# A speech joint network's forward and backward pass: gradient rows transposed by DMA, one weight-gradient tap moved an iteration on, row loads on another queue

## The chip, the cores and the metric

The kernel runs on one core of one Trainium2 chip. The metric is device time in microseconds (us) of one execution; lower is better. The engines are named as in the profile: PE is TensorE (PEld its weight loads), DVE VectorE, ACT ScalarE, POOL GpSimd, SP SyncE. SP computes nothing here and issues DMAs. A DMA that SP issues and one that POOL issues go through different queues (in the profile q1 hardware_dynamic and q0 software_dynamic).

## The reference

Two strided convolutions with gelu, a projection, and a joint over U = 8 label positions; the outputs are the forward result and the gradients of all seven inputs. B = 2, T = 16000, D = 256, three taps, all bf16.

```python
def _fwd_reference(x, w1, w2, g, w_f, w_g, w_o):
    ...
    h = _gelu(h)[:, ::2, :]          # h: three taps of x with w1
    ...
    f = _gelu(f)[:, ::2, :]          # f: three taps of h with w2
    fe = jnp.einsum("btd,de->bte", f, w_f)
    ge = jnp.einsum("bud,de->bue", g, w_g)
    j = jnp.tanh(fe[:, :, None, :] + ge[:, None, :, :])
    return jnp.einsum("btud,dv->btuv", j, w_o)

def reference(x, w1, w2, g, w_f, w_g, w_o, grad_out):
    ...
    _out, _vjp = jax.vjp(_f, x, w1, w2, g, w_f, w_g, w_o)
    _grads = _vjp(grad_out)
    _out0 = jnp.asarray(_out)
    return (_out0, *[jnp.asarray(_g) for _g in _grads])
```

The gradient through the tanh, summed over the eight label positions, is what the rest of the backward pass starts from. The kernel keeps it with its sign turned and calls it NGFE.

## The kernel before

**Tiling.** Time after both strides has 4000 positions per batch. Both batches stand one after the other in one axis with a gap of 16, cut into 16 chunks of 512 columns (the last has 336; the eighth, n = 7, holds the end of the first batch and the start of the second, so each of its transfers falls into several pieces). Channels lie on partitions, 2 x 128.

**The main loop** runs over the chunks n. One iteration does three things at once: the joint of chunk n (four steps of two label positions each), the two convolutions and the projection of chunk n + 1, and the backward pass of chunk n - 1. The joint is the generator `main`; the other two are chained into the generator `fill`, and `weave` takes one unit of `fill` after nearly every unit of `main`. A scheduler then orders each engine's instructions, mostly along that order. After the loop the backward pass of the last chunk runs alone.

**The joint.** `gj` squares the tanh (ACT), multiplies grad_out, transposed (tile GOT), by w_o (PE, L635) and makes the gradient NGZ of one label position (DVE, L639, three buffers). `ngfe_acc` sums the NGZ on POOL (L658); the eighth sum is written as NGFE (one buffer). `o_block` is the forward matmul (L695), its result OUT is copied by ACT and stored by POOL's queue (L722). `gwo` is the gradient of w_o (L734): it needs the tanh with time on partitions (JR, transposed by a DMA of SP's queue, L667, two buffers) and grad_out's rows (GO, loaded by SP's queue in `load_go`, L202, three buffers). Both are asked for at a step's start or end and read one step after their own joint.

**The backward pass of a chunk**, in order: `d1_units` multiplies NGFE by w_f (L431) and makes GF (DVE, L433). `row_units` transposes what the weight gradients need with time on partitions: first NGFE (8 matmuls against the identity into one PSUM bank, L467, one DVE copy, L469), then four sets of 6 or 8 (HT and GF, copied by ACT). `d5_units` goes back through w2 (L454) and makes GH. `braid` alternates the two, beginning with the NGFE unit. `gwf_units` is the w_f gradient (L512; its rows are FR, transposed by DMA, and the NGFE rows), `gw2_units` that of w2 (L530). `ghr_units` transposes GH (16 matmuls, L467). `e_units` makes the x gradient (`gx_block`, L590, four per chunk, copied to GX by ACT, stored by POOL) and the three taps of the w1 gradient (`gw1`, 16 matmuls each, L603). `gw1` reads the GH rows and XR, rows of x that POOL's queue loads (`load_xr`, L213, one buffer, four pieces in the first two steps of the next iteration). The third tap stands between the third and the fourth `gx_block`, at the end of the iteration.

**Buffers.** Pool `rowp` (five buffers, tile "rows") holds the NGFE rows, the four HT/GF sets and the two GH sets of a chunk in turn.

**Queues.** SP's and POOL's instructions run in order, so a DMA issue that waits for a buffer or for data holds up all that is behind it in its queue. POOL's queue mixes sums, small copies, stores and loads.

Of the kernel before, what the change touches and what calls it, by code (L numbers as in the profile page):

```python
# [13 lines left out]
BF16 = mybir.dt.bfloat16  # L14
# [8 lines left out]
P = 128  # L23
KT = 2
KK = 3
# [3 lines left out]
CW = 512  # L29
# [3 lines left out]
def kernel(  # L33
# [30 lines left out]
    def geom(n):  # L64
        c0 = n * CW
        return c0, min(CW, L - c0)
# [43 lines left out]
    accp = pool("accp", 1)  # L110
    gfp = pool("gfp", 2)
    ghp = pool("ghp", 2)
    rowp = pool("rowp", 5)
    xrp = pool("xrp", 1)
    gxp = pool("gxp", 2)
    jtp = pool("jtp", 4)
# [75 lines left out]
    def joint_dram(t, b, q, m, up, nb):  # L192
        src = t[b, q:q + m, 2 * up:2 * up + 2, :]
        return src.rearrange("(tb p) u v -> p tb (u v)", tb=nb)

    def load_go(n, up):
        t = gop.tile([P, 4, 2 * V], BF16, name="GO")
        for lo, hi in gaps(n):
            p0 = lo % P // 32 * 32
            nc.vector.memset(t[p0:-(-(hi % P) // 32) * 32, lo // P, :], 0.0)  # L200
        for b, q, m, p0, p1, k, nb in joint_rows(n):
            nc.sync.dma_start(out=t[p0:p1, k:k + nb, :], in_=joint_dram(grad_out, b, q, m, up, nb))  # L202
        S[n]["GO", up] = t


# [257 lines left out]
    def transposes(srcs, dsts, evict=None):  # L463
# [4 lines left out]
        for dst, M, j0, j1 in dsts:  # L468
            (evict or nc.vector.tensor_copy)(out=dst, in_=ps[:M, j0:j1, :])  # L469

    def load_fr(n):
        W = geom(n)[1]
        FR = frp.tile([P, KT, 4, P], BF16, name="FR")
        nc.sync.dma_start_transpose(out=FR[:].rearrange("p k a d -> p (k a) d"),
                                    in_=S[n]["FT"][:].rearrange("p k w -> p (k w)"))
        S[n]["FR"] = FR

    def row_units(n):
        c0, W = geom(n)
        st = S[n]  # L480
        HT, GF, FT, NG = st["HT"], st["GF"], st["FT"], st["NGFE"]
        bl = blocks(W)
        FR = st["FR"]
        t = rowp.tile([P, 8, P], BF16, name="rows")
        st["NR"] = t
        srcs = [(NG[:, kt, o:o + M], 2 * j + kt, M) for j, (o, M) in enumerate(bl) for kt in range(KT)]
        dsts = [(t[:M, 2 * j:2 * j + 2, :], M, 2 * j, 2 * j + 2) for j, (o, M) in enumerate(bl)]
        if W == CW:
            dsts = [(t[:], P, 0, 8)]
        transposes(srcs, dsts)  # L490
        yield
        st["HG"] = []
        s = nsets(n)
        for k, M in sets(n):
            t = rowp.tile([P, 8, P], BF16, name="rows")
            col = lambda off: slice(off + k, off + k + s * (M - 1) + 1, s)
            srcs = [(HT[:, par, kt, col(2)], 2 * par + kt, M) for par in range(2) for kt in range(KT)]
            srcs += [(GF[:, kt, col(2)], 4 + kt, M) for kt in range(KT)]
            if k == 0:
                srcs += [(HT[:, 1, kt, col(1)], 6 + kt, M) for kt in range(KT)]  # L500
            transposes(srcs, [(t[:M, 0:len(srcs)], M, 0, len(srcs))], nc.scalar.copy)
            st["HG"].append(t)
            yield

    def gwf_units(n):
        W = geom(n)[1]
        FR, t = S[n]["FR"], S[n]["NR"]
        bl = blocks(W)
        ps = ps_f32()
        for k, (o, M) in enumerate(bl):  # L510
            for dt in range(KT):
                nc.tensor.matmul(ps[:, dt * D:(dt + 1) * D], lhsT=FR[:M, dt, k, :],  # L512
                                 rhs=t[:M, 2 * k:2 * k + 2, :].rearrange("p k d -> p (k d)"),
                                 start=(k == 0 and dt == 0), stop=(k == len(bl) - 1 and dt == KT - 1))
        flush("F", ACCF[:], ps[:])
        first_flush["F"] = False
        yield
# [17 lines left out]
        first_flush["2"] = False  # L535

    def braid(rows, d5):
        for gen in (rows, d5, rows, d5, rows, d5, rows, rows, d5):
            yield next(gen, None)

    def alternate(a, b):
# [31 lines left out]
    def e_units(n):  # L573
        st = S[n]
        s = nsets(n)
        GH, GR, XR = st["GH"], st["GR"], st["XR"]
        bl = back_sets(n)

        def gx_block(k, M):
            t = gxp.tile([P, 4, D], BF16, name="GX")  # L580
            combos = (((0, 1, 0), (2, 0, -1)), ((1, 1, 0),), ((2, 1, 0), (0, 0, 0)), ((1, 0, 0),))
            for cp in range(2):
                ps = ps_f32()
                for cj in range(2):
                    cc = combos[2 * cp + cj]
                    j, last = 0, len(cc) * KT - 1
                    for (i, par, sh) in cc:
                        for kt in range(KT):
                            o = 2 + k + sh
                            nc.tensor.matmul(ps[:M, cj * D:(cj + 1) * D], lhsT=GH[:, par, kt, o:o + s * (M - 1) + 1:s],  # L590
                                             rhs=W1T[:, i, kt, :], start=(j == 0), stop=(j == last))
                            j += 1
                nc.scalar.copy(out=t[:M, 2 * cp:2 * cp + 2, :], in_=ps[:M, :])  # L593
                yield
            store_gx(n, k, t)

        def gw1(i):
            ps = ps_f32()
            for j, (k, M) in enumerate(bl):
                t, g = GR[j]  # L600
                for dt in range(KT):
                    for par in range(2):
                        nc.tensor.matmul(ps[:, dt * D:(dt + 1) * D],  # L603
                                         lhsT=XR[:M, 4 * k + i + 2 * (1 - par), dt * P:(dt + 1) * P],
                                         rhs=t[:M, g + 2 * par:g + 2 * par + 2, :].rearrange("p k d -> p (k d)"),
                                         start=(j == 0 and dt == 0 and par == 0),
                                         stop=(j == len(bl) - 1 and dt == KT - 1 and par == 1))
            flush("1", ACC1[:, i, :], ps[:])

        for j, (k, M) in enumerate(bl):  # L610
            yield from gx_block(k, M)
            if j < KK:
                gw1(j)
                yield
        first_flush["1"] = False


# [206 lines left out]
        tanh(0, u)  # L824
    load_jr(0, 0)

    for n in range(G):
        back, fwd = n > 0, n + 1 < G
        conv = conv_units(n + 1) if fwd else iter(())
        conv2 = conv2_units(n + 1) if fwd else iter(())  # L830
        late_open[0] = False
        parts = []
        if back:
            d1, e, rows, ghr = d1_units(n - 1), e_units(n - 1), row_units(n - 1), ghr_units(n - 1)
            parts += [islice(conv, 2), islice(d1, 1), islice(conv, 1), d1, conv, braid(rows, d5_units(n - 1)),
                      gwf_units(n - 1), gw2_units(n - 1), islice(ghr, 1), islice(conv2, 1), ghr, conv2, islice(e, 6)]
            if fwd:
                parts.append(fe_units(n + 1))
            parts.append(e)
        else:  # L840
            parts += [conv, empty(3), islice(conv2, 1), empty(3), conv2, empty(3), fe_units(n + 1)]
        fill = chain(*parts)
        ratio = (0.92 if n > 0 else 0.4) if n + 1 < G else 0.72
        for up in range(U // 2):
            step = n * (U // 2) + up
            if step + 2 < len(orderp):
                load_got(*orderp[step + 2])
            if step + 1 < len(orderp):
                load_go(*orderp[step + 1])
            if up == 1:  # L850
                load_fr(n)
            for piece in (((0,), (1,), (2, 3), ()) if n == G - 1 else ((0, 1), (2, 3), (), ()))[up] if back else ():
                load_xr(n - 1, piece)
            main = joint_units(n, up)
            weave(main, fill, ratio)
            if up == U // 2 - 1:
                for _ in fill:
                    pump(2)
                    pump_late(1)
                pump(len(later))  # L860
                late_open[0] = True
                pump_late(len(late))
            for i in range(2):
                if 2 * step + 2 + i < len(order):
                    tanh(*order[2 * step + 2 + i])
            if step + 1 < len(orderp):
                load_jr(*orderp[step + 1])
            if n + 2 < G:
                load_x(n + 2, ((0,), (1,), (), ())[up])
# [2 lines left out]
        gwo(*prev_gwo[0], k)  # L872
    for piece in range(4):
        load_xr(n, piece)
    for _ in chain(d1_units(n), alternate(row_units(n), d5_units(n)), gwf_units(n), gw2_units(n), ghr_units(n), e_units(n)):
        pass


# [71 lines left out]
```

## Time and profile before

| | us |
|---|---|
| median of 3 runs | 839.2 |
| lowest, highest | 837.9, 847.22 |
| the profiled execution | 834.64 |
| its span in the profile | 832.7 |

| Group (line, engine) | count | mean ns of one | busy us |
|---|---|---|---|
| L734 PE, w_o gradient | 1008 | 274 | 150.0 |
| L695 PE, forward joint | 1008 | 274 | 148.7 |
| L603 PE, w1 gradient | 756 | 273 | 90.4 |
| L467 PE, transposes of NGFE | 126 | 219 | 9.6 |
| L469 DVE, copies of transposes | 51 | 647 | 32.7 |
| L658 POOL, sums | 80 | 2111 | 168.9 |
| L722 POOL, OUT stores | 76 | 737 | 55.9 |

| DMA | issuer | size KB | median us from issue to landing |
|---|---|---|---|
| GO | SP | 512 | 5.4 |
| GOT, transposing | SP | | 7.7 |
| JR, transposing | SP | | 6.8 |
| FR, transposing | SP | | 4.5 |
| XR | POOL | 256 | 7.1 |
| OUT | POOL | 512 | 6.0 |

How to read it: matmuls are pipelined, so the mean duration of one (274 ns) is longer than the distance from one to the next, and the chain of waits, which counts from start to start, gives four L734 matmuls 0.44 us and eight transposes 0.45 us. A DMA's landing is counted from its issue. An issue's own duration is the time that its queue is taken. Small groups and the waits' releasers are inferred from semaphores.

### The profile page before, as it was taken

To read this page: it belongs to the slowest core of one execution; us is meant where nothing else is said; L and a number is where in the kernel's file an instruction comes from. 1 tells how busy PE (TensorE), PEld (TensorE's weight loads), DVE (VectorE), ACT (ScalarE), POOL (GpSimd) and SP (SyncE) were. 2 spreads that over 40 slices of the span, in tenths; PEclk is the share of its full clock that TensorE was granted. 3 is DMA by queue.
4 is the path that set the end of the run, shared out by engine and by line. 5 is a ranking of instruction groups with operands and counts; after the bars stand their busy time and mean duration, and the time that the engine had idled before them with its cause. 6 is when DMAs were issued, how large, how long until landed. Compare 5 with 4: busy or idle time off the path is not lost.

```text
span 832.7 us, 16683 instructions
## 1 busy us (share of the span) xinstructions
PE 809.9 (97%) x6396; PEld 600.1 (72%) x6396; DVE 627.5 (75%) x1211; ACT 678.8 (82%) x1080; POOL 402.0 (48%) x423
## 2 busy tenths in 40 slices
PE   7979999999999999999999999999999999999797
PEld 3546777768678676777768678677777868778596
DVE  4896797886869778696877869778696886878344
ACT  3889998796979969799797979969798896978344
POOL 1154644454544535545477545535544454556371
PEclk9999999999999999999999999999999999999999
DMA  9878999999999999999999999999999999998954
GB/s 215 193 180 185 221 223 264 224 254 231 246 245 221 195 250 246 238 240 194 231 246 248 264 235 260 254 230 245 220 246 230 233 252 240 224 230 186 213 139 131
DMA packets 395344, 187.88 MB, mean 226 GB/s; under 512 B 343296, under 2 KB 379032, under 8 KB 395264
## 3 DMA queue, kind: packets, MB, share of 16 engines
q1 hardware_dynamic: 374944, 119.69, 77.3%
q0 software_dynamic: 20320, 67.12, 26.1%
q8 instruction: 50, 0.82, 0.4%
q14 instruction: 30, 0.25, 0.1%
HBM read 51.38 MB, written 50.34 MB: 122 GB/s over the span
## 4 chain that ended last, share of the span: by engine, by line
PE 84%; ACT 6%; DVE 5%; DMA 3%; issue 1%; POOL 0%; POOLq 0%; DVEq 0%; ACTq 0%
PE GWO_ps L734 12%; PE ps L695 11%; PE ps L635 11%; PE ps L603 9%; PE ps L590 9%; PE ps L324 7%; PE ps L530 5%; PE pst L467 5%; PE ps L359 5%; PE ps L454 4%; DMA JR<-JT 3%; PE ps L512 2%; ACT JT L401 2%; PE ps L383 2%; PE ps L431 1%; DVE g_s L264 1%
## 5 line engine op out<-in xcount | busy, mean ns | idle before, releaser
L639 DVE SCALAR_TENSOR_TENSOR NGZ<-JSQ,ps 128x512 bf16<-128x512 bf16 (+3 forms) x272 | 168.1, 639 | 45.1 <-PE ps L635 39.3
L658 POOL TENSOR_TENSOR ACCN<-ACCN,NGZ 128x1024 f32<-128x1024 f32 (+1 forms) x80 | 168.9, 2111 | 68.0 <-DVE NGZ L639 67.2
L697 ACT CAST OUT<-ps 128x512 bf16<-128x512 f32 (+1 forms) x252 | 146.1, 596 | 41.2 <-PE ps L695 36.0
L401 ACT ACTIVATE JT<-FE,GE 128x512 bf16<-128x512 f32 (+3 forms) x272 | 176.8, 710 | 0.5
L627 ACT ACTIVATE JSQ<-JT 128x1024 bf16<-128x1024 bf16 (+1 forms) x128 | 135.1, 1059 | 37.8 <-DVE NGZ L639 37.8
L734 PE MATMUL GWO_ps<-GO,JR 128*128 128x256 bf16 (+1 forms) x1008 | 150.0, 274 | 7.8 <-DMA JR<-JT 5.7
L695 PE MATMUL ps<-WO,JT 128*128 128x256 bf16 (+1 forms) x1008 | 148.7, 274 | 0.0
L722 POOL DMA_DIRECT2D out_dram<-OUT x76 | 55.9, 737 | 183.5 <-ACT OUT L697 171.2
L635 PE MATMUL ps<-GOT,WOT 128*128 128x512 bf16 (+1 forms) x512 | 139.0, 376 | 0.0
L734 PEld LDWEIGHTS <-JR 128*128 128x128 bf16 (+1 forms) x1008 | 97.3, 98 | 34.8 <-DMA JR<-JT 6.4
L695 PEld LDWEIGHTS <-JT 128*128 128x128 bf16 (+1 forms) x1008 | 98.0, 99 | 21.6 <-issue 1.3
L590 PE MATMUL ps<-W1T,GH 128*128 128x256 bf16 (+2 forms) x756 | 100.4, 273 | 0.0
L590 PEld LDWEIGHTS <-GH 128*128 128x128 bf16 (+2 forms) x756 | 83.5, 116 | 13.0
L324 PE MATMUL ps<-XC,W 128*128 128x512 bf16 (+1 forms) x384 | 91.1, 375 | 0.0
L603 PE MATMUL ps<-rows,XR 128*128 128x256 bf16 (+1 forms) x756 | 90.4, 273 | 0.0
L415 DVE TENSOR_TENSOR ACC<-ACC,ps 128x512 f32<-128x512 f32 x90 | 61.5, 684 | 37.9 <-PE ps L530 26.4
L264 DVE SCALAR_TENSOR_TENSOR g_s<-g_sq,g_x 128x1024 bf16<-128x1024 bf16 (+2 forms) x35 | 69.9, 1998 | 25.3 <-ACT g_sq L264 25.3
L603 PEld LDWEIGHTS <-XR 128*128 128x128 bf16 (+1 forms) x756 | 73.9, 98 | 11.6
L593 ACT CAST GX<-ps 128x512 bf16<-128x512 f32 (+2 forms) x126 | 72.3, 588 | 11.2 <-PE ps L590 4.8
L245 POOL DMA_DIRECT2D out_dram<-GX x67 | 36.8, 550 | 82.7 <-ACT GX L593 77.7
L635 PEld LDWEIGHTS <-WOT 128*128 128x128 bf16 x512 | 48.4, 98 | 32.4 <-issue 0.8
L324 PEld LDWEIGHTS <-W 128*128 128x128 bf16 x384 | 37.4, 98 | 37.3
(132 smaller groups left out, 1235.4 us busy)
## 6 DMA issues: line engine op xcount, KB each, us to landing
GO<-in_grad_out_dram SPq DMA_DIRECT2D x56, 512.0 KB, 5.4
out_dram<-OUT POOLq DMA_DIRECT2D x56, 512.0 KB, 6.0
out_dram<-GX POOLq DMA_DIRECT2D x55, 256.0 KB, 4.6
XR<-in_x_dram POOLq DMA_DIRECT2D x39, 256.0 KB, 7.1
XR<-in_x_dram POOLq DMA_DIRECT2D x13, 320.0 KB, 7.6
GO<-in_grad_out_dram SPq DMA_DIRECT2D x4, 384.0 KB, 4.1
out_dram<-OUT POOLq DMA_DIRECT2D x4, 384.0 KB, 6.1
GOT<-in_grad_out_dram SPq DMA_TRANSPOSE x68, 7.7
```

The costliest lines, as they stand in the source:

```text
L264: later.popleft()()
L324: nc.tensor.matmul(ps[:, :W], lhsT=W1[:, i, kt, mt * P:(mt + 1) * P], rhs=st["X", c][:, kt, 16 + sh:16 + sh + W], start=(k == 0), stop=(k ...
L401: act = nc.scalar.activation(out=JT[:, mt, lo:hi], in_=S[n]["FE"][:, mt, lo:hi], func=ACT.Tanh, bias=GE[:, b, mt, u:u + 1], scale=1.0)
L590: nc.tensor.matmul(ps[:M, cj * D:(cj + 1) * D], lhsT=GH[:, par, kt, o:o + s * (M - 1) + 1:s], rhs=W1T[:, i, kt, :], start=(j == 0), stop=( ...
L603: nc.tensor.matmul(ps[:, dt * D:(dt + 1) * D], lhsT=XR[:M, 4 * k + i + 2 * (1 - par), dt * P:(dt + 1) * P], rhs=t[:M, g + 2 * par:g + 2 * ...
L627: jsq = nc.scalar.activation(out=JSQ[:, :, :W], in_=JT[:, :, :W], func=ACT.Square)
L635: nc.tensor.matmul(ps[:, :W], lhsT=WOT[:, kt, mt * P:(mt + 1) * P], rhs=GOT[:, kt, :W], start=(kt == 0), stop=(kt == KT - 1))
L639: nc.vector.scalar_tensor_tensor(out=NGZ[:, mt, lo:hi], in0=JSQ[:, mt, lo:hi], scalar=1.0, in1=ps[:, lo:hi], op0=ALU.subtract, op1=ALU.mul ...
L658: st["last"] = nc.gpsimd.tensor_tensor(out=out, in0=in0, in1=st["NGZ", u][:, :, :W], op=ALU.add)
L695: nc.tensor.matmul(ps[:M, j * V:(j + 1) * V], lhsT=st["JT", u][:, kt, o:o + M], rhs=WO[:, kt, :], start=(kt == 0), stop=(kt == KT - 1))
L697: nc.scalar.copy(out=OUT[:M, k, :], in_=ps[:M, :])
L734: nc.tensor.matmul(GWO_ps[:, dt, :], lhsT=JR[:M, j, dt, k, :], rhs=GO[:M, k, j * V:(j + 1) * V], start=(n_gwo[0] == 0), stop=(n_gwo[0] == ...
```

## The change

Three edits.

1. For all chunks but the last, NGFE's rows come from a DMA transpose on SP's queue (`load_nr`, the same call as FR's, both now made by `load_rows`) into a tile of its own (pool `nrp`, one buffer), called at the start of the next iteration, ahead of that step's other loads. `row_units` does the PE transposes only where no such tile is there, which is the last chunk; its copies by DVE then write the new layout. `rowp` has four buffers in place of five, and `braid` one unit fewer.
2. The third w1 tap comes last in `e_units`, behind the fourth `gx_block`. The iteration takes only the four units ahead of it (two `gx_block`), and the tap, left in `rest`, is placed in the next iteration's `fill` between the convolution and `braid`; after the loop it stands ahead of the last chunk's backward pass.
3. `load_go` issues on POOL's queue in place of SP's.

```diff
-    rowp = pool("rowp", 5)
+    rowp = pool("rowp", 4)
+    nrp = pool("nrp", 1)
...
-            nc.sync.dma_start(out=t[p0:p1, k:k + nb, :], in_=joint_dram(grad_out, b, q, m, up, nb))
+            nc.gpsimd.dma_start(out=t[p0:p1, k:k + nb, :], in_=joint_dram(grad_out, b, q, m, up, nb))
...
+    def load_rows(pool_, name, src):
+        t = pool_.tile([P, KT, 4, P], BF16, name=name)
+        nc.sync.dma_start_transpose(out=t[:].rearrange("p k a d -> p (k a) d"), in_=src.rearrange("p k w -> p (k w)"))
+        return t
+
     def load_fr(n):
...
+        S[n]["FR"] = load_rows(frp, "FR", S[n]["FT"][:])
+
+    def load_nr(n):
+        S[n]["NR"] = load_rows(nrp, "NR", S[n]["NGFE"][:])
...
-        t = rowp.tile([P, 8, P], BF16, name="rows")
-        st["NR"] = t
...
-        transposes(srcs, dsts)
-        yield
+        if "NR" not in st:
+            t = nrp.tile([P, KT, 4, P], BF16, name="NR")
+            st["NR"] = t
+            ps = ps_bf()
+            for j, (o, M) in enumerate(bl):
+                for kt in range(KT):
+                    nc.tensor.transpose(out=ps[:M, 4 * kt + j, :], in_=NG[:, kt, o:o + M], identity=ident[:])
+            for j, (o, M) in enumerate(bl):
+                nc.vector.tensor_copy(out=t[:M, :, j, :], in_=ps[:M, j:j + 5:4, :])
+            yield
...
-                                 rhs=t[:M, 2 * k:2 * k + 2, :].rearrange("p k d -> p (k d)"),
+                                 rhs=t[:M, :, k, :],
...
-        for gen in (rows, d5, rows, d5, rows, d5, rows, rows, d5):
+        for gen in (rows, d5, rows, d5, rows, d5, rows, d5):
...
             yield from gx_block(k, M)
-            if j < KK:
+            if j < KK - 1:
                 gw1(j)
                 yield
+        gw1(KK - 1)
+        yield
...
+    rest = iter(())
...
-            parts += [islice(conv, 2), islice(d1, 1), islice(conv, 1), d1, conv, braid(rows, d5_units(n - 1)),
+            parts += [islice(conv, 2), islice(d1, 1), islice(conv, 1), d1, conv, rest, braid(rows, d5_units(n - 1)),
...
-            parts.append(e)
+            parts.append(islice(e, 4))
+            rest = e
...
+            if back and up == 0:
+                load_nr(n - 1)
...
-    for _ in chain(d1_units(n), alternate(row_units(n), d5_units(n)), gwf_units(n), gw2_units(n), ghr_units(n), e_units(n)):
+    for _ in chain(rest, d1_units(n), alternate(row_units(n), d5_units(n)), gwf_units(n), gw2_units(n), ghr_units(n), e_units(n)):
```

More of the change, by code (lines that the diff above doesn't have):

```diff
@@ L469, in transposes @@
             (evict or nc.vector.tensor_copy)(out=dst, in_=ps[:M, j0:j1, :])
+    def load_rows(pool_, name, src):
+        t = pool_.tile([P, KT, 4, P], BF16, name=name)
+        nc.sync.dma_start_transpose(out=t[:].rearrange("p k a d -> p (k a) d"), in_=src.rearrange("p k w -> p (k w)"))
+        return t
     def load_fr(n):
[L472 to L476, printed above, removed]
+        S[n]["FR"] = load_rows(frp, "FR", S[n]["FT"][:])
+    def load_nr(n):
+        S[n]["NR"] = load_rows(nrp, "NR", S[n]["NGFE"][:])
     def row_units(n):
@@ L483, in row_units @@
         FR = st["FR"]
-        t = rowp.tile([P, 8, P], BF16, name="rows")
-        st["NR"] = t
[L486 to L489, printed above, removed]
-        transposes(srcs, dsts)
-        yield
+        if "NR" not in st:
[8 more added lines that the diff above has]
+            yield
         st["HG"] = []
```

## The prediction

> **What bounds the kernel now.** I read the page's first two parts first. Part 1 gives each engine's busy time and share of the span, part 2 the span in 40 slices.
>
> ```profile
> span 832.7 us, 16683 instructions
> PE 809.9 (97%) x6396; PEld 600.1 (72%) x6396; DVE 627.5 (75%) x1211; ACT 678.8 (82%) x1080; POOL 402.0 (48%) x423
> ...
> PE   7979999999999999999999999999999999999797
> ```
>
> TensorE (PE) has gaps at the two ends only. A busy PE need not be a paced PE, so next comes the chain of waits in order of time, cut to one ordinary iteration (start, length, what):
>
> ```profile
> 219.55 0.86 PE ps L635 x4
> ...
> 227.34 1.29 PE ps L324 x6
> 228.64 0.44 PE GWO_ps L734 x4
> 229.07 0.45 PE pst L467 x8
> 229.52 0.44 PE ps L695 x4
> ...
> 251.01 1.75 PE ps L603 x16
> ...
> 261.91 1.75 PE ps L603 x16
> ...
> 269.32 0.86 PE ps L635 x4
> ```
>
> From one iteration's first L635 to the next's it is 49.77 us, and every piece between is a matmul group standing end to end: no wait, no other engine. In such a stretch a matmul removed is time removed. The eight "pst L467" at 229.07 are the transposes of the summed tanh gradient (NGFE); the L603 group at 261.91 is the third w1 tap.
>
> Then the few places where PE does stop. The waits of the whole span (total us, times, longest us) name one releaser for a middle or late stop, JR, the transposed tanh rows that the w_o gradient (L734) reads:
>
> ```profile
> PE GWO_ps L734 <- DMA JR<-JT: 5.7, 2, 5.3
> ```
>
> The chain shows its larger case near the end, and SyncE's (SP's) queue shows what was ahead of it:
>
> ```profile
> 765.61 17.09 DMA JR<-JT
> ```
> ```profile
> 755.96 2.08 SPq L667 DMA_TRANSPOSE JR<-JT  x1
> 758.10 3.00 SPq L202 DMA_DIRECT2D GO<-in_grad_out_dram  x2
> 761.35 1.51 SPq L174 DMA_TRANSPOSE GOT<-in_grad_out_dram  x1
> 765.61 6.18 SPq L667 DMA_TRANSPOSE JR<-JT  x1
> ```
>
> That transfer took 17.09 us against a median of 6.8 (part 6), and PE stood 5.33 us for it. The queues' packet time is 77.3% and 26.1% of 16 engines' span, so the DMA engines have little to spare.
>
> **The change, part by part.** *Transposes of NGFE leave PE.* In 15 of the 16 iterations (all chunks but the last, which keeps the PE path) eight transposes go, 0.45 us each time: 15 x 0.45 = 6.75 us off PE, in a chain that is all PE. DVE loses 15 evictions of 0.66 us, off the path. A transpose by SP's queue comes instead; its like is FR, same shape, 1.25 us of issue and 4.5 us to landing. It waits for NGFE on GpSimd (POOL), whose sum ended at 219.54 and at 269.31; the JR queued behind it on SP was issued at 219.87 and 269.81, so NGFE is there when its turn comes and JR is pushed back by the 1.25 us of issue. JR: 269.81 + 1.25 + 6.8 = 277.9, first read by L734 at 288.57, 10 us of cover. The rows themselves: 269.8 + 4.5 = 274.3, read by L512 at 287.69, 13 us of cover. Without that cover either would cost its lateness in each iteration. I take -6.75, and bounds of -6.75 and 0 (0 if PE's pace were given by another engine, below).
>
> *The third tap moves* (16 matmuls, 1.75 us, 15 times) from an iteration's end to the place where the transposes stood. PE's total is unchanged, so 0. It also covers what the transposes covered: GF, evicted by DVE until 228.56, is needed by the next matmuls; the 1.75 us stand in front of them, where 0.45 us stood. On the last chunk the tap lands before L431 in the tail, where PE has no gap: 0 as well. But it holds two things longer. The two "rows" buffers of the GH transposes are held into the next iteration with 4 buffers in place of 5: the third set of transposes is the first to need one, and it stands behind the tap in PE's order, so 0. And the x rows (XR, one buffer) can be reloaded only after the tap. These loads are on POOL, and POOL now stops at the first of them until the tap ends, 229.07 + 1.75 = 230.8; behind it queue an OUT store, a GO load, two more XR loads and the NGZ sums. The first pair was issued at 222.35, the second at 233.07 to 234.15. Now: 230.8 + 1.08 (XR) + 0.78 (OUT) + 0.77 (GO) + 1.08 (XR) = 234.5, and OUT was not ready before 232.30 anyway: 235.0. With the median 7.0 us to landing that is 242.0; the first tap reads at 251.01 - 0.45 = 250.6. Cover 8.6 us: 0 in ordinary iterations. In the iteration of the chunk that spans both batches there is also a memset of 3.89 us and 13 XR pieces of 0.54 us: tap's end near 431.1 + 3.9 + 0.8 (OUT) + 7.0 + 0.8 (GO) = 443.6, + 7.0 = 450.6, read at about 451.34 - 0.45 = 450.9. Bounds 0 and +8 (the longest XR landing, 15.1 us); I take +1, as the median just fits and the pieces queue on one another.
>
> *GO's loads go to POOL* (76 issues). POOL pays at most the OUT row's 0.77 us each (same 512 KB, same 1 KB runs), 3.1 us per iteration on 24.2 busy of 52: not a bound. Each load is queued behind the OUT store of the step before, which waits for ACT; GO is read one and a half steps, about 18 us, after its issue and lands in 5.4, so its lateness costs 0. At the start, though, three loads (1.5 MB) are now issued right behind the weights, by about 6.5 us, where the first was at 11.23 on SP; the conv input XC is then still in flight (SP issues it until 6.27, landing 4.7 to 7.5) and the conv starts at 9.60. [...] I take +1: 1.4 us of the conv's wait is the WG load's, which stays ahead of GO.
>
> *SP loses GO and gains NR.* Ahead of the late JR stood 3.00 us of GO issues; 1.25 us of NR take their place: JR 1.75 us earlier, so -1.75. Bounds: -5.7 (both JR stalls gone) and +3 (GO, now in POOL's ring beside XR and OUT, slows that JR as much as its own issue had).
>
> [...]
>
> Sum: -6.75 + 1 + 1 - 1.75 = -6.5 us. The profiled execution took 834.64 us (its span is 832.7), so 828.1 there. The median of the runs shown is 839.2, 4.6 above it; the terms are differences, so I carry them over: 839.2 - 6.5 = 832.7.
>
> **The rivals.**
> *A, the forecast:* PE keeps the pace and small costs stay small, 828 to 837. Chance 0.48.
> *B, the DMA side gets freer:* the unprofiled runs are 3.3 to 12.6 us longer than the profiled one, and the late JR is the kind of stop that could make them so. If SP's shorter queue removes these, -6.75 - 5.7 and some 2 of the 4.6 us: 839.2 - 14.5 = 824.7. For it: the 17.09 us. Against: the full DMA engines. 0.24.
> *C, slower: the x rows are late.* XR's reload behind the tap, with GO ahead of its second pair in POOL's queue and ring, lands after the first tap wants it. It decides once landing takes more than 8.6 us over the median, 15.6 us, or POOL's issue is held as long. At 17 us PE stops 1.4 us in 14 iterations: 832.7 + 20 = 853. For it: 15.1 us did occur once in 77; against: the median 7.0. [...]
>
> ```profile
> L722 POOL DMA_DIRECT2D out_dram<-OUT x76: 518/770/816, 41.0 to 809.0; - x76
> ```
>
> These are shortest, median and longest in ns: not one of 76 issues was held. C has 0.16, of which 0.03 for the held issues. [...]
> *D, no gain:* the removed matmuls leave holes because ACT (43.1 to 44.7 us busy in ordinary stretches of 52) or NGFE's arrival sets the pace. Then 839 to 841. Against: no ACT piece in the ordinary chain. 0.12.
>
> **How the numbers follow.** About 1% is what a measurement of this kernel can tell from no change: 830.8 to 847.6. Faster by more: all of B and a third of A, 0.24 + 0.16 = 0.40. Slower by more: C, 0.16. The rest, 0.44, lies within. The range leaves out half of B's low tail and C from about 845 up: 822 to 845.
>
> **What would show it.** Ordinary iterations of 49.3 us in the chain, with no L467 on NGFE before the last chunk; L603 groups of 16 behind the last L324 of the next iteration; NR landing near 4.5 us; no wait of L603 for XR (C otherwise) except near 450 us; the first L324 later than 9.6 us by about 1 us; the late JR shorter than 17 us. An iteration that stays at 49.8 us would show the forecast's main term wrong (D).

## The result, and the profile after

| | before | after |
|---|---|---|
| median, us | 838.6 (6 runs) | 919.8 (6 runs) |
| lowest, highest | 835.9, 847.2 | 892.4, 941.8 |
| the profiled execution, its span | 834.6, 832.7 | 892.4, 890.6 |

The change makes the kernel slower. The times of one kernel scatter here, the more the slower it is, so ratios are taken from the undisturbed runs near each kernel's fastest: 1.064, with a 95% interval of 1.055 to 1.073. In medians it is 81 us.

The page of the changed kernel, its first two parts (busy time and share of the span; then forty slices, in tenths):

```profile
span 890.6 us, 16460 instructions
...
PE 817.1 (92%) x6211; PEld 598.9 (67%) x6276; DVE 625.8 (70%) x1196; ACT 680.5 (76%) x1080; POOL 459.2 (52%) x499
...
PE   7979895899999999999798894999999999799997
...
PEclk9989997899999999999999997999999999899999
```

PE had gaps at the ends only; now it has holes in the middle, each some slices wide, and stretches at 9 between them. In five slices the granted clock is lower too, 7 or 8 tenths where the others have 9, and PE is below 9 in each of the five. What PE waits for (total us, times, longest us):

```profile
PE GWO_ps L743 <- DMA JR<-JT: 41.3, 9, 11.4
PE ps L610 <- DMA XR<-in_x_dram: 3.8, 3, 2.0
...
PE ps L519 <- DMA NR<-NGFE: 2.2, 1, 2.2
```

Lines are 1 to 13 higher than before: L743 is the w_o gradient (L734), L610 the w1 gradient (L603), L676 JR (L667). JR was 5.7 us in 2 waits; it is 41.3 in 9. The x rows of rival C are a fifteenth of the 57.9 us that this execution is longer. The chain of waits over the whole span, its long pieces (start, length, what):

```profile
99.48 10.21 DMA JR<-JT
...
133.53 24.74 DMA JR<-JT
...
199.40 1.75 PE ps L610 x16
248.72 1.75 PE ps L610 x16
...
316.30 8.55 DMA JR<-JT
...
419.64 10.38 DMA JR<-JT
...
512.07 16.13 DMA JR<-JT
...
597.57 10.05 DMA JR<-JT
...
740.25 22.68 DMA JR<-JT
```

The two L610 groups are the moved tap of two successive chunks: 49.32 us apart, where the iteration before took 49.77. So what the forecast says of PE is there, in an iteration in which nothing goes wrong. In others a JR of 8 to 25 us sits on the path. For the seven shown, the tanh was done 10 us or more and the buffer free 5 us or more before SP issued the load, so neither of these is what made it late. Issues and median landing, of the answer on DMAs:

```profile
GO<-in_grad_out_dram POOLq DMA_DIRECT2D x56, 512.0 KB, 7.7
...
JR<-JT SPq DMA_TRANSPOSE x60, 9.3
...
NR<-NGFE SPq DMA_TRANSPOSE x15, 7.1
```

JR was 6.8, GO on SP 5.4. And SP's queue around the longest JR (start, us that the issue took), with the busy times of the same stretch (PE, PEld, DVE, ACT, POOL, granted clock, the DMAs' packet time, GB/s):

```profile
117.20 3.45 SPq L676 DMA_TRANSPOSE JR<-JT  x1
120.85 9.70 SPq L175 DMA_TRANSPOSE GOT<-in_grad_out_dram  x1
130.65 2.77 SPq L474 DMA_TRANSPOSE NR<-NGFE  x1
133.53 13.83 SPq L676 DMA_TRANSPOSE JR<-JT  x1
147.45 10.59 SPq L175 DMA_TRANSPOSE GOT<-in_grad_out_dram  x1
```
```profile
128.00:136.00 8.00, 7.96 (x57) 5.42 (x57) 4.46 (x10) 7.60 (x13) 3.18 (x5) 1.00 1.40 151
136.00:158.00 22.00, 9.44 (x74) 6.03 (x72) 8.36 (x17) 11.98 (x18) 8.06 (x10) 0.74 1.08 182
158.00:164.00 6.00, 5.69 (x29) 4.10 (x30) 1.04 (x2) 0.00 (x0) 0.00 (x0) 0.52 1.18 239
164.00:172.00 8.00, 7.94 (x63) 5.50 (x62) 4.32 (x10) 3.19 (x5) 2.91 (x3) 1.00 1.02 230
```

SP's issues stand end to end here, and each takes 3 to 14 us. No two of its issues overlap in either trace (207 here, 268 before, at the least 0.04 us apart), so a long one holds up all that stand behind it. Over the whole trace an issue of JR takes 4.3 us in the median and 13.8 at most, where before it took 3.2 and 6.8. I take it that the transfers ahead hold the queue up, which is not shown: for the issue of 13.83 us the profile names only a copy of OUT by ACT, which JR does not read. From 136 to 158 PE works 9.44 of 22 us, and for six us behind that it runs at about half the clock (0.52).

A whole run can be laid out by iteration: the distances in the trace from the first w_o gradient matmul of one chunk to that of the next. The fifteenth and last distance is another: it runs to the last such matmul of all, so it holds the last two chunks. "First" is what lies ahead of the first of these matmuls, "rest" what comes behind the last.

| kernel | first | distances, us | rest |
|---|---|---|---|
| before | 33.3 | 56.0 49.8 49.8 49.8 49.8 49.8 50.6 50.4 49.8 49.8 49.8 49.8 49.8 48.0 73.8 | 22.9 |
| after | 35.4 | 56.5 66.5 51.9 49.3 49.3 50.3 51.0 57.7 60.4 63.2 50.5 49.3 49.3 58.0 67.1 | 25.0 |

The sum of the distances grew by some 54 us of the span's 57.9. No steady amount is added: ten distances are at most 2.1 us above their counterparts of before, some below, and five (66.5, 57.7, 60.4, 63.2, 58.0) carry the loss, 58 us together. (The last distance is 66.5 to 66.7 in four other profiles without a late load there, so the 73.8 of before holds the late JR that the prediction showed.)

### The profile page after: what moved, and what is told of

Same layout as the page of the kernel before. It is cut to its first block, busy times and chain, and to the rows that moved or that the text cites. A ratio compares the mean times of both kernels' runs of the same rounds, so it can differ in the third digit from the quotient of the medians.

```text
span 890.6 us, 16460 instructions
## 1 busy us (share of the span) xinstructions
PE 817.1 (92%) x6211; PEld 598.9 (67%) x6276; DVE 625.8 (70%) x1196; ACT 680.5 (76%) x1080; POOL 459.2 (52%) x499
## 4 chain that ended last, share of the span: by engine, by line
PE 61%; DMA 16%; ACT 9%; DVE 7%; issue 3%; POOL 2%; SPq 1%; DVEq 0%; POOLq 0%; ACTq 0%
DMA JR<-JT 12%; PE GWO_ps L743 10%; PE ps L704 8%; PE ps L644 8%; PE ps L597 7%; PE ps L610 7%; PE ps L325 6%; PE ps L537 4%; ACT JT L402 3%; PE ps L360 3%; PE pst L468 3%; PE ps L455 3%; DVE NGZ L648 2%; ACT OUT L706 1%; ACT JSQ L636 1%
## 5 line engine op out<-in xcount | busy, mean ns | idle before, releaser
L743 PE MATMUL GWO_ps<-GO,JR 128*128 128x256 bf16 (+1 forms) x1008 | 153.8, 279 | 44.9 <-DMA JR<-JT 41.3
L667 POOL TENSOR_TENSOR ACCN<-ACCN,NGZ 128x1024 f32<-128x1024 f32 (+1 forms) x80 | 169.3, 2117 | 43.3 <-DVE NGZ L648 42.4
L743 PEld LDWEIGHTS <-JR 128*128 128x128 bf16 (+1 forms) x1008 | 98.3, 100 | 73.9 <-DMA JR<-JT 44.6
L597 PE MATMUL ps<-W1T,GH 128*128 128x256 bf16 (+2 forms) x756 | 103.0, 277 | 0.0
L610 PE MATMUL ps<-rows,XR 128*128 128x256 bf16 (+1 forms) x756 | 94.3, 279 | 3.8 <-DMA XR<-in_x_dram 3.8
L597 PEld LDWEIGHTS <-GH 128*128 128x128 bf16 (+2 forms) x756 | 84.4, 117 | 14.2
L265 DVE SCALAR_TENSOR_TENSOR g_s<-g_sq,g_x 128x1024 bf16<-128x1024 bf16 (+2 forms) x35 | 62.8, 1793 | 42.8 <-ACT g_sq L265 42.8
L610 PEld LDWEIGHTS <-XR 128*128 128x128 bf16 (+1 forms) x756 | 75.6, 100 | 15.3 <-DMA XR<-in_x_dram 4.6
```

Source lines behind the costliest of these rows:

```text
L610: nc.tensor.matmul(ps[:, dt * D:(dt + 1) * D], lhsT=XR[:M, 4 * k + i + 2 * (1 - par), dt * P:(dt + 1) * P], rhs=t[:M, g + 2 * par:g + 2 * ...
L667: st["last"] = nc.gpsimd.tensor_tensor(out=out, in0=in0, in1=st["NGZ", u][:, :, :W], op=ALU.add)
L743: nc.tensor.matmul(GWO_ps[:, dt, :], lhsT=JR[:M, j, dt, k, :], rhs=GO[:M, k, j * V:(j + 1) * V], start=(n_gwo[0] == 0), stop=(n_gwo[0] == ...
```

## The experiments

Each row's median is over all its runs, in us, beside that of the kernel before on the same chip; a ratio stands where there is an interval for it.

**Which part it is.** First the parts, alone and left out. T1 to T4 are the theories: GO beside the transposes, NGFE's transpose ahead of JR, the tap, and only both DMA moves together.

go_sp, the changed kernel with GO on SP again:

```diff
-            nc.gpsimd.dma_start(out=t[p0:p1, k:k + nb, :], in_=joint_dram(grad_out, b, q, m, up, nb))
+            nc.sync.dma_start(out=t[p0:p1, k:k + nb, :], in_=joint_dram(grad_out, b, q, m, up, nb))
```

> The changed kernel with grad_out's rows (GO) issued by SP again; the DMA transpose of NGFE and the moved tap stay. T1 (GO beside the transposes, in POOL's queue, slows SP's transposing loads): the loss goes, 828 to 838, JR landing back near 6.8 us (9.3 in the changed kernel), PE's wait for JR below 8 us (41.3). T2 (the transpose of NGFE, put ahead of JR in SP's order, delays JR): still slow, 870 to 900. T3 (the moved tap holds POOL's queue and the x rows): still slow, 860 or more, with waits of L610 for XR. T4 (only GO and NR together overload the transfers): 828 to 838 as well, told from T1 by GO alone.

go_only, the kernel before with the opposite of that line:

> The kernel before with only GO's loads moved to POOL's queue. T1: most of the loss, 875 to 925, JR landing 9 us or more, PE's wait for JR 30 us or more (5.7 before). T2 and T3: 837 to 842, no change but for the start. T4: 838 to 855.

nr_only, the kernel before with `load_nr`, `load_rows`, the pools and the new `braid`, the tap in its old place, GO on SP:

> The kernel before with only the DMA transpose of NGFE (and its pool and four rows buffers); GO on SP, the third tap in its old place. T1: 832 to 840: up to 6.75 us off PE, of which the wait for GF, which the transposes covered, takes up to 1 us in each of 15 iterations. T2: 870 to 900, JR landing late. T3: as T1. T4: 832 to 845.

tap_only, the kernel before with the tap moved:

```diff
-            if j < KK:
+            if j < KK - 1:
                 gw1(j)
                 yield
+        gw1(KK - 1)
+        yield
...
-            parts.append(e)
+            parts.append(islice(e, 4))
+            rest = e
```

> The kernel before with only the third w1 tap moved into the next iteration (five rows buffers, NGFE transposed on PE, GO on SP). T1, T2, T4: 835 to 843. T3: 860 or more, L603 waiting for XR or its issue held on POOL.

| kernel | median | before | ratio |
|---|---|---|---|
| go_sp | 863.4 | 843.7 | 1.017 (1.007 to 1.027) |
| go_only | 867.7 | 843.7 | 1.023 (1.012 to 1.033) |
| nr_only | 861.3 | 843.7 | 1.025 (1.015 to 1.036) |
| tap_only | 841.8 | 843.7 | 1.002 (0.998 to 1.007) |

No theory holds alone. T3 falls: the tap is free. GO alone costs 24 us and NGFE's transpose alone 18, and together with the tap they cost 81. In the medians that is more than their sum; in the ratios it is 6.4% against 2.3, 2.5 and 0.2, with an interval of a point to either side of the larger ones, so that it is more than a sum is not shown. go_sp, go_only and nr_only all wait for JR: go_only 14.2 us, nr_only 16.3 and go_sp 30.0 in their profiles, where before has 5.7. go_only has three long ones in its chain:

```profile
107.26 14.55 DMA JR<-JT
...
345.50 21.98 DMA JR<-JT
...
801.20 21.79 DMA JR<-JT
```

**Was there anything to gain on PE?** In these profiles the time in which any packet of q0 or q1 was in flight (787 us of 832.7 in before, 847 of 890.6 in after, 820 of 857.4 in nr_only) is the span less some 40 us, so the next theory, D2, was that the transfers as such set the pace; D1 is the forecast's own. no_nr takes the PE transposes away and puts nothing in their place:

```diff
-        transposes(srcs, dsts)
-        yield
...
-                                 rhs=t[:M, 2 * k:2 * k + 2, :].rearrange("p k d -> p (k d)"),
+                                 rhs=FR[:M, :, k, :],
```

> The kernel before without the transposes of NGFE and their DVE copies, and with nothing in their place; the w_f gradient multiplies FR by FR's own rows, so it is not the reference's. D1 (PE sets the pace, as the forecast's main term has it): 6.75 us less, ratio 0.992. D2 (the transfers set the pace as much as PE: the time in which any packet was in flight plus some 40 us is the span in all six profiles so far): no gain, ratio 0.998 to 1.003.

Measured: 838.0 against 837.2, ratio 1.002 (0.996 to 1.008). The forecast's term alone would be 0.992, below the interval, so most of the 6.75 us does not arrive. Its iterations say why:

| kernel | first | distances, us | rest |
|---|---|---|---|
| no_nr | 33.5 | 56.9 49.3 49.3 49.3 49.3 49.3 50.5 51.7 49.4 54.9 49.3 49.3 49.3 48.1 73.7 | 22.7 |

The quiet ones take 49.3, so the term is right there; one iteration of 54.9, with a JR that PE waits for, and one of 51.7 took most of it back in this execution.

**NGFE's transpose as a load.** nr_unused leaves all PE work of before and only adds the transpose, unread (seven eighths of it):

```diff
+    def load_nr(n):
+        t = nrp.tile([P, 7, P], BF16, name="NR")
+        nc.sync.dma_start_transpose(out=t[:], in_=S[n]["NGFE"][:].rearrange("p k w -> p (k w)")[:, :7 * P])
...
+            if back and up == 0:
+                load_nr(n - 1)
```

> The kernel before with all its PE work, and in addition a DMA transpose of seven eighths of NGFE on SP's queue at the place where the change has it, 15 times, whose result nothing reads. D2, or SP's order delaying JR: 850 to 862, as much as the transpose cost where it was used (861 median). D1 with a cost only through the use of NR (PE waits at L519): 838 to 842.

nr_late issues it two steps later (`up == 2`). O is the theory that its place in SP's order, ahead of JR, is what costs:

> As the kernel before with the unread DMA transpose of seven eighths of NGFE, but issued at the start of the iteration's third step instead of the first, so that other JR loads are behind it. D2 (load): 850 to 866 as at the first place (862.7 median). O: another time than there; if NGFE's lateness or the first step's JR were the point, 836 to 845.

swap exchanges the two operands of the w_f gradient, so that the number of DMA transposes and of PE transposes is that of before:

```diff
-        srcs = [(NG[:, kt, o:o + M], 2 * j + kt, M) for j, (o, M) in enumerate(bl) for kt in range(KT)]
+        TR = NG if n == G - 1 else FT
+        srcs = [(TR[:, kt, o:o + M], 2 * j + kt, M) for j, (o, M) in enumerate(bl) for kt in range(KT)]
...
+            if back and up == 0:
+                S[n - 1]["NR"] = load_rows("NR", S[n - 1]["NGFE"])
```

> The kernel before with the two rows of the w_f gradient exchanged: NGFE goes through the DMA transpose on SP's queue at the change's place, FT through the eight PE transposes (all chunks but the last). The load on the transfers and PE's work are those of before; only the place in SP's order is the change's. D2 (load): within 1% of before, 834 to 846. O (order: NGFE's transpose stands ahead of JR and waits for POOL): 855 or more.

| kernel | median | lowest to highest | before | ratio |
|---|---|---|---|---|
| nr_unused | 862.7 | 855.7 to 878.6 | 837.2 | 1.033 (1.022 to 1.043) |
| nr_late | 849.5 | 843.6 to 861.7 | 838.7 | 1.013 (1.007 to 1.019) |
| swap | 854.6 | 836.1 to 860.4 | 838.7 | none |

The transpose costs 25 us though nothing reads it. In the profile of nr_unused (878.6 us, the longest of its four runs):

```profile
PE GWO_ps L739 <- DMA JR<-JT: 35.9, 8, 11.4
```

At another place it costs 11; with as many DMA transposes as before but at the change's place 16 in the median, with one run of four at no loss. So the load and the place both count, and swap alone would not settle either.

**GO's queue.** go_act moves GO to ACT, another hardware queue (q10 hardware_dynamic in its answer on DMAs, 32.77 MB, where SP's is q1):

```diff
-            nc.sync.dma_start(out=t[p0:p1, k:k + nb, :], in_=joint_dram(grad_out, b, q, m, up, nb))
+            nc.scalar.dma_start(out=t[p0:p1, k:k + nb, :], in_=joint_dram(grad_out, b, q, m, up, nb))
```

> The kernel before with GO issued by ACT in place of SP or POOL. G1 (POOL's software queue is what makes GO slow the others): 836 to 846. G2 (any queue beside SP's lets GO run in turns with the transposes, which lengthens each JR): 850 to 870, JR landing 8 us or more, as with POOL (867.7 median, 8.8 us). Start: the conv's first L324 later than in before in both.

872.7 against 838.7, ratio 1.043 (1.036 to 1.050). GO and JR in its answer on DMAs:

```profile
GO<-in_grad_out_dram ACTq DMA_DIRECT2D x56, 512.0 KB, 5.6
...
JR<-JT SPq DMA_TRANSPOSE x60, 9.5
```

G1 falls: it is not POOL's software queue. JR is as late with a second hardware queue. (PE also waits 9.4 us once for a copy by ACT and 5.4 us for GO, and the first conv matmul starts at 14.6 us in place of 9.6, so the ratio is not JR's alone.)

go_mid and after_go_mid try to keep GO on POOL but out of JR's way:

```diff
+        step = n * (U // 2) + up
+        if step + 1 < len(orderp):
+            load_go(*orderp[step + 1])
```

(behind the second `gwo` of a step, in place of the call at its start)

> The kernel before with GO on POOL's queue, but issued in the middle of a step, behind the sums, so that it flies when JR, asked for at the step's start, has landed; the program order is kept for it. G2 (GO in flight beside JR lengthens JR): JR's median back below 7.5 us (8.8 with GO issued at the step's start), 836 to 850. G3 (the same bytes through POOL's queue cost more whenever they fly): 855 to 870.

> The changed kernel with GO on POOL's queue issued in the middle of a step. G2: only what NGFE's transpose costs remains, 855 to 870. G3: 885 to 925 as with the change.

917.4 against 842.0, ratio 1.082 (1.069 to 1.096), and 926.7. Both missed. The move did not do what it was to do: of 44 JR loads whose landing the trace has, 28 still had a GO in flight for over 2 us (39 in go_only), landing in 9.5 us in the median, the other 16 in 6.1. So it tells only that half a step later is worse, not why.

What the trace gives without a new kernel is the split of JR's landings by that overlap, medians in us: go_only 9.2 with GO in flight (39 loads) and 6.1 without (5), go_act 9.7 (29) and 7.6 (12), after 10.0 (37) and 5.7 (11). In before, where GO stands in the same queue as JR, it is 7.1 (24) and 6.2 (20), and with an overlap of 1 us as the bound 6.5 and 7.1: no clear difference. (GO's own landing is missing for a quarter of its loads in before and go_act.) It is a coincidence in time, not a trial, but the three kernels with GO on another queue agree. Whether the two queues take turns, as G2 has it, no run here shows.

**Bytes in flight.** Four kernels leave transfers out, two add some. before_no_out and after_no_out store OUT for the last chunk only:

```diff
+            if n == G - 1:
-            nc.gpsimd.dma_start(out=joint_dram(out_0, b, q, m, up, nb), in_=OUT[p0:p1, k:k + nb, :])
+                nc.gpsimd.dma_start(out=joint_dram(out_0, b, q, m, up, nb), in_=OUT[p0:p1, k:k + nb, :])
```

> The kernel before without the stores of OUT for all chunks but the last (some 31 of 188 MB of packets less; the first output stays unwritten there). D1: within 1% of before, PE having had no idle time to lose but 5.7 us at JR: 828 to 838. D2: 820 to 832, PE then the only bound.

> The changed kernel without the stores of OUT for all chunks but the last. D2 (the loss is the transfers' load): the loss goes, and the 6.75 us of the forecast come out against the kernel before without these stores: 818 to 832. If the loss is SP's order (NR ahead of JR) or GO's place in POOL's instruction order, it stays for the most part: 860 to 900.

no_nr_no_out takes the PE transposes away from the first of these:

> The kernel before without the stores of OUT for all chunks but the last and without the transposes of NGFE (the w_f gradient takes FR's rows twice). D1 and D2 both: with the transfers relieved PE sets the pace and the 6.75 us come out, 819 to 823 against 827.6 with the transposes. If PE was not the pace even there: 826 to 829.

after_no_xr and after_no_gx take away half as many bytes, once the loads of x rows and once the stores of GX:

```diff
+        if n > 0:
+            S[n]["XR"] = S[0]["XR"]
+            return
```
```diff
     def store_gx(n, k, t):
+        if n < G - 1:
+            return
```

> The changed kernel without the loads of x rows for all chunks but the first, whose rows stand in for the others (the w1 gradient is not the reference's); some 15 MB of transfers less. In the traces so far the transposes move 121 GB/s where only an XR load is in flight beside them, against 166 with OUT, 178 with GX and 219 alone. J1 (the long JR transfers come from the transposes flying beside XR): most of the loss goes, 825 to 840. J2 (bytes in flight, whichever): about half of what the stores of OUT were worth, 860 to 885.

> The changed kernel without the stores of the x gradient for all chunks but the last (out_1 stays unwritten there): about as many bytes less as in the run without XR. J1: the loss stays for the most part, 870 to 915. J2: as without XR, 860 to 885.

| kernel | median | lowest to highest | before | ratio |
|---|---|---|---|---|
| before_no_out | 827.6 | 825.9 to 829.4 | 837.2 | 0.991 (0.988 to 0.994) |
| no_nr_no_out | 825.2 | 824.1 to 826.4 | 842.0 | 0.983 (0.977 to 0.988) |
| after_no_out | 834.5 | 829.8 to 859.2 | 837.2 | 0.998 (0.995 to 1.002) |
| after_no_xr | 837.7 | 828.5 to 870.4 | 845.8 | 0.997 (0.990 to 1.004) |
| after_no_gx | 861.7 | 838.1 to 884.2 | 845.8 | 0.998 (0.989 to 1.007) |

Without the OUT stores the changed kernel's loss of 81 us is gone. PE's waits there:

```profile
PE ps L610 <- DMA XR<-in_x_dram: 5.6, 2, 4.6
...
PE GWO_ps L744 <- DMA JR<-JT: 0.9, 1, 0.9
```

JR's waits are gone, though its median landing is still 8.2. But it does not come out 6.75 below before_no_out, as expected of it; it stays 7 above. In the two profiles (832.2 and 826.9) the fourteen distances of single chunks are 4.2 us shorter in sum, the last distance 7.2 longer (73.8, with a late XR) and the rest 2.2 longer. Whether no_nr_no_out gives the whole term where everything is quiet stays open: its median is 2.4 us below that of before_no_out and its profile 4.6 (822.3, with one iteration of 51.4 in place of 49.8), but the two ran on different chips, and each against before on its own chip they are 9.6 and 16.8 us faster, which is 7.2 apart. Without XR's loads the median is lower than without GX's stores, at about 16 MB each, but the ranges overlap widely, the ratios are alike, and without XR's loads POOL no longer stops behind the tap either (11.0 us in 11 stops in after). So bytes count, as J2 has it; that XR counts beyond its bytes (J1) is not shown.

The other direction, unread plain loads of x rows by POOL; first two per iteration:

```diff
+    def extra(n):
+        t = extp.tile([P, 896], BF16, name="EXTRA")
+        nc.gpsimd.dma_start(out=t[:], in_=x_rows(x, 0, 1024 * (n - 1), P, 7, 8)[:, :896])
...
+            if back and up in (0, 2):
+                extra(n)
```

> The kernel before with two unread plain loads of x rows of 224 KB more per iteration (30 in all, 6.9 MB), issued by POOL; nothing is added to SP's queue. At the 250 GB/s that the trace moves in stretches with plain loads alone they are 27 us of transfers. D2: 850 to 866. O, or a limit in SP's queue alone: 836 to 845.

905.3 against 838.7, ratio 1.085 (1.075 to 1.094), in the range of no theory, and no test of any. The loads depend on nothing but their one buffer, and the scheduler had put them all at the front (shortest, median and longest issue in ns; first and last start in us):

```profile
L481 POOL DMA_DIRECT2D EXTRA<-in_x_dram x30: 536/539/604, 4.1 to 137.1; - x30
```

POOL stood behind them, and the first distance is 79.0 us where before has 56.0. So plain_kept holds one per iteration to its place:

```diff
-        nc.gpsimd.dma_start(...)
+        tc.keep_in_program_order(nc.gpsimd.dma_start(...))
...
-            if back and up in (0, 2):
+            if back and up == 2:
```

> The kernel before with one unread plain load of 224 KB of x rows more per iteration by POOL, held to its place in the order (15 in all, 3.4 MB, 14 us of transfers at the 250 GB/s of plain loads alone). D2 (any load on the transfers costs): 846 to 862. If only SP's queue is the limit: 836 to 843.

837.5 against 842.0, ratio 0.992 (0.987 to 0.998): no cost.

```profile
EXTRA<-in_x_dram POOLq DMA_DIRECT2D x15, 224.0 KB, 6.2
...
JR<-JT SPq DMA_TRANSPOSE x60, 6.7
```

D2, that any load costs, falls with it. Some 14 us of transfers (an estimate: 3.4 MB at 250 GB/s; stretches of 1 us without transposes in the trace of before move 233 in the median) went in and the span did not grow; the time with packets in flight stayed at 787 us. That that time is the span less some 40 us in the kernels with all their transfers is no sign of a limit: without OUT's stores it is the span less 95 us or more. But 3.4 MB at one place are a ninth of OUT's 31 MB, and taking those away did help. So I read it that load matters as far as it makes JR late, not by its amount alone.

**JR's cover.** So the common measure is JR's own: from the trace, for each of the 60 loads, the time from its issue to the first matmul that reads it, its landing where the trace has it (43 to 48 loads), and the difference. Medians in us, and how many landings took over 12 us:

| kernel | issue to use | landing | cover left | over 12 us |
|---|---|---|---|---|
| before | 15.1 | 6.8 | 8.2 | 1 of 44 |
| plain_kept | 16.7 | 6.7 | 9.6 | 0 of 44 |
| nr_unused | 13.1 | 7.0 | 5.5 | 6 of 43 |
| go_only | 16.7 | 8.8 | 7.9 | 6 of 44 |
| after | 14.0 | 9.3 | 4.5 | 10 of 48 |
| after_no_out | 16.9 | 8.2 | 8.0 | 8 of 48 |

NGFE's transpose takes cover at one end: in nr_unused JR has 2 us less from issue to use. GO takes it at the other: in go_only JR lands 2 us later, though the median cover hardly moves, since JR also has 1.6 us more from issue to use; what PE meets are the long landings, 6 in place of 1. The change does both, the cover is 4.5 in place of 8.2, and long landings come through to PE. Where OUT's stores are gone they are still there (8 of 48) but find 8 us of cover, and PE waits 0.9 us.

The median hides which load has least. An iteration has four JRs. In before, the one that comes to stand right behind NGFE's transpose has 17.2 us from issue to use in the median; the next one, behind the XC loads (the conv input, transposed), has 12.0, and 6.1 at the least. In after, 28 of the 41 us that PE waits for JR are at this second one, in six of the nine waits. In nr_unused the waits are spread over three of the four.

## Why the prediction was wrong, point by point

*PE bounds the kernel, and a matmul removed is time removed.* True of a quiet iteration, to the hundredth: 49.77 to 49.32. Not true of the kernel: no_nr removed the same matmuls, put nothing in their place and showed no gain (1.002). The chain of before was read from one execution with two JR stops; it was 4 us faster than the median run, which may have had more of them.

*The transpose by SP's queue.* This is the step that failed. It said that JR is pushed back by 1.25 us of issue and then has 10 us of cover, and priced the rest at 0. The 1.25 us were right for the issue of NR alone (1.24 in nr_unused), but the other issues of the queue grew (JR's from 3.2 to 3.6 us there), and JR had 2 us less on its way to its use. And the 10 us set a median landing against one use, and of the load with the most time. SP's rows of before, in the same iteration:

```profile
269.81 3.17 SPq L667 DMA_TRANSPOSE JR<-JT  x1
...
293.48 2.93 SPq L667 DMA_TRANSPOSE JR<-JT  x1
```

The first is the one that the prediction took, read 19 us after its issue; the next JR is read 10 us after its own, which leaves 3 us beside the median landing. The median cover over the run was 8.2, with a landing of 17.09 us in the very rows that the prediction showed. The packet time of 77.3% and 26.1%, which it read as little to spare, told nothing of this: plain_kept added 3.4 MB at no cost (0.992). Measured price of the step: 25 us (nr_unused), against a term of -6.75 with 0 as its upper bound. (nr_only, which has both the transpose and the gain on PE, lost 18; the 7 us between them are the size of the term, but the intervals overlap.) NR itself landed in 7.1 us, not 4.5, and was waited for once, 2.2 us; its 13 us of cover held.

*The third tap, 0.* Right: 1.002 (0.998 to 1.007). In the profile of tap_only its ordinary iterations are 50.13 us, 0.4 more than before; in the changed kernel 49.32, where the transposes next to it are gone. The iteration with the x rows of the chunk that spans both batches, priced at +1 with +8 as its bound, took 55.2 in tap_only with XR in the chain, against 49.8 before, so +1 was too small there; in after it took 60.4, with a landing of OUT that POOL waited for, stores of GX and a JR of 16.1 us in the chain.

*GO to POOL: lateness 0, POOL no bound.* Both right: no wait of PE names GO, and POOL is 52% busy. The start, +1: no run shows this term. The conv input's second load landed at 11.93 us in place of 9.07, the first conv matmul came at 9.98 us in place of 9.60 and the first w_o gradient 2.1 us later, but in other kernels with GO on SP they come as late (up to 10.8 and 36.1), so no cost of it is shown in the change. go_only has 11.5 and 37.1, so some of GO's price there may be the start's.

*SP loses GO, -1.75, at worst +3.* Wrong in sign and size. It took GO's issue time as what delayed JR. What GO's place in SP's queue did, as I read the split of JR's landings, was to keep its 512 KB behind JR. On POOL it costs 24 us (go_only), on ACT 34. The bound of +3 priced one late JR; there were several.

*The rivals.* C had the sign but not the cause: XR was worth 3.8 us of waits, JR 41.3. (As a load beside JR it counts for more: without its loads the median is 837.7, in after_no_xr.) Nor was one of POOL's issues held in the changed kernel: those of OUT took 0.80 us at most, those of XR 0.60. B's late JR became the rule instead of going away. D asked for iterations that stay at 49.8, and they did not. The case that came, JR late several times for two reasons, was in no rival, though its two halves stood in the text as costs of 0 and as a bound of +3.

What stays open: why single JR loads take 15 to 25 us when the median is 9, which of their neighbours does it, whether GO's price is all its flight beside JR (go_mid failed to part them), and whether the two DMA moves cost more together than their sum.

## What to carry to other kernels

Before work is moved to a DMA queue, find the load in that queue with the least cover, over the whole trace and not in one iteration, and set its longest landings against that cover, not its median. Treat the order of loads in one queue as a priority: a load taken out of it may no longer wait behind the urgent one but fly beside it, as GO did here (JR landed in 8.8 us in the median with GO on POOL's queue and 9.5 with it on ACT's, against 6.8). And a term that is right in a quiet iteration is worth nothing if it is bought with a transfer that makes one iteration in three unquiet.

## What the runs showed of the hardware that was not expected

- 224 KB more per iteration as a plain load on POOL's queue cost nothing (0.992), 224 KB more as a DMA transpose on SP's cost 25 us over 15 iterations at the first step (nr_unused) and 11 at the third, where the plain load stood (nr_late). Kind of transfer and queue change together here, so which of the two it is stays open.
- Counted in bins of 1 us in nine profiles with GO on SP, the transposes moved some 215 GB/s with none of the other loads and stores in flight, 180 with GX alone, 150 to 165 with OUT alone, and 110 to 120 with XR alone, where all transfers together made only 175 to 185. The figures depend on how a bin is assigned, by up to a third; XR's stays the lowest and the one without other transfers the highest.
- Behind the stop of PE at 136 us the granted clock stayed low: 0.74 in the 22 us of the stop, 0.52 in the 6 us after it with PE busy 5.69 of them, then 1.00. Four matmuls of the w_o gradient took 0.83 us from start to start at 158.31 and 0.43 at 164.87. So this stop cost PE some time beyond its own length. In go_only it was 0.92 in the 22 us from 345, 0.72 in the 6 us after with PE busy 5.47 of them, then 1.00.
